# Sigmoid attention and a gated MLP on one core: 24 sums of token halves made by GpSimd instead of VectorE

## The chip, the cores and the metric

The kernel runs on one core of a Trainium2 chip. The metric is the device time of one execution in microseconds. The core's engines work through their own lists of instructions in order, and wait for each other by semaphores: TensorE (PE in the profile, with its weight loads as PEld), VectorE (DVE), ScalarE (ACT), GpSimd (POOL) and SyncE (SP), which here issues the stores.

## The reference

For 8 batches, 12 heads, 448 tokens and a head dimension of 64, attention with a sigmoid in place of the softmax is followed by a gated MLP on 3584 tokens of width 768, with a hidden width of 2048:

```
scores = q @ k.T / sqrt(64) - log(448)
x      = sigmoid(scores) @ v                # heads side by side: 3584 x 768
h      = x @ w_in                           # 3584 x 2048
g      = h * sigmoid(beta * h)
out    = g @ w_out                          # 3584 x 768, float32
```

## The kernel before

**Tiling.** Attention works on groups of 4 heads of one batch (24 groups, g = 3b to 3b+2 for batch b). Scores are made transposed (keys on partitions), ScalarE takes the sigmoid out of PSUM (L225), and the products with v give x transposed, which VectorE copies as f16 into the tile `xT` of the batch (128 x 6 x 448: six blocks of 128 features by 448 tokens, L294). Layer one then gives the hidden units on partitions in `gt`, and layer two gives token tiles of 128 rows, in pairs, which SyncE stores.

**Seven products instead of eight.** For batches 2 to 7, layer one is done by a Strassen-like scheme (Winograd's form): both operands are cut into halves, sums of halves are made first, and seven products P1 to P7 replace eight. The sums of the weights (`w_S`, `w_T`) are made once. The sums of the token halves are made for every batch by `token_sum(b, i)`, four to a batch, 24 in all: each takes two f16 blocks of 128 x 672 elements (3 features' blocks by 224 tokens) from SBUF and writes a third. With b11, b12, b21 and b22 the quarters of `xT` (features by tokens) they are, in this order or with the last two exchanged:

- sum 0: t0 = b12 - b11, read by product P5
- sum 1: t1 = b22 - t0, read by P6
- sum 2: b12 = b22 - b12, in place in `xT`, read by P7
- sum 3: t2 = b21 - t1, read by P4

t0, t1 and t2 lie in the tile `xs`, of which there is one buffer: the next batch's sum 0 waits for the last readers of this batch's. Products P1, P2 and P3 read no sum made here. Layer two uses the same scheme on pairs of token tiles; its sums of hidden halves (`hidden_sum`, tile `sum`, 128 x 1024, f16) are made by VectorE from `gt`.

**Order.** The order of all work behind a short prologue is one list of steps written out by hand. Every engine gets its instructions in the order of this list. The names of the steps that matter:

- Xb.i: `token_sum` of batch b, sum i
- Ib.d.p: product p of layer one for the d-th quarter of the hidden units (L433 by way of L166), with its eviction (L453 on ScalarE, L455 to L472 on VectorE, or sigmoids L415 on ScalarE)
- Gb.d and Bb.d.j: sigmoids on ScalarE (L415) and then the gate's product on GpSimd (L482 and L492), which writes `gt`
- Ht.i: `hidden_sum` on VectorE; Ut.p.part: half of product p of layer two for the tiles t and t+1, with its eviction
- Qg and Kb: loads of q and k of a group (two transfers) and of v of a batch (six), all issued by GpSimd (L110, L131, L138)
- Vg.j: scores of a group and their sigmoids; Ag: the product with v and its two copies into `xT`; Rg.r: transposes of q and k on VectorE; Eb: a copy of rows of v on VectorE

The stretch of the list around batch 5's first sums:

```
        V18.2 I4.3.4 B4.3.1 X5.0 A17 B4.3.0 I5.0.1 G4.3 Q21 X5.1 U14.1.0 V18.1 I5.0.2 I5.0.6 U14.1.1
        I5.0.5 V18.0 U14.2.0 H14.0 H14.1 I5.0.3 H14.2 U14.2.1 X5.2 X5.3 V18.3 U14.6.0 E6 U14.6.1
```

**PSUM.** In this part four banks are shared by all products of TensorE but the scores. `bank` takes the bank that has been free longest in the order of the list, so a product that opens a bank waits for the eviction that emptied it: I7.0.5 takes the one that U20.3.1 leaves, and U18.1.0 the one of U16.4.1.

**Helper.** `add` (L361, L362) is the VectorE operation on two inputs behind the sums of weights, of tokens and of hidden halves, and behind most evictions. In the profile all of them have the line L362, and are told apart by their tiles.

Of the kernel before, what the change touches and what calls it, by code (L numbers as in the profile page):

```python
# [13 lines left out]
def kernel(  # L14
# [10 lines left out]
    nc = tc.nc  # L25
    AF = mybir.ActivationFunctionType
    ALU = mybir.AluOpType
# [333 lines left out]
    def add(out, in0, in1, op=ALU.add):  # L361
        nc.vector.tensor_tensor(out=out, in0=in0, in1=in1, op=op)  # L362
# [36 lines left out]
    def token_sum(b: int, i: int):  # L399
        x = xTs[b]  # L400
        b11, b12 = x[:, 0:NK, 0:QH], x[:, 0:NK, QH:S]
        b21, b22 = x[:, NK:NHC, 0:QH], x[:, NK:NHC, QH:S]
        if i == 0:
            xs[b] = xsp.tile([P, 3, NK, QH], FP16, tag="xs", name="xs")
        t = xs[b]
        out, in0, in1 = (
            (t[:, 0], b12, b11),
            (t[:, 1], b22, t[:, 0]),
            (b12, b22, b12),
            (t[:, 2], b21, t[:, 1]),  # L410
        )[i]
        add(out, in0, in1, ALU.subtract)

    def sigmoid(out, in_, dc: int):
        nc.scalar.activation(  # L415
# [181 lines left out]
    def first_half(n: int):  # L597
# [13 lines left out]
        "Q": load_qk,  # L611
        "K": load_v,
        "X": token_sum,
        "G": weigh_right,
        "B": weigh_below,
# [74 lines left out]
    with tc.manual_schedule():  # L690
# [6 lines left out]
        for r, c0, c1 in early:  # L697
# [3 lines left out]
                out=staged[r],  # L701
# [113 lines left out]
```

## Time and profile before

| what | value |
|---|---|
| median of 3 runs | 372.45 us (372.42 to 374.46) |
| the profiled execution | 372.17 us, of it the span from first to last instruction 370.4 us |
| TensorE busy | 363.1 us (98%) |
| VectorE busy | 271.2 us (73%) |
| ScalarE busy | 246.9 us (67%) |
| GpSimd busy | 147.7 us (40%), 186 instructions |
| the 24 token sums on VectorE | 12.1 us, about 0.5 us each |
| the 52 hidden sums on VectorE | 37.7 us, 0.68 us each as a rule |
| the 72 gate products on GpSimd | 81.6 us, 1.14 us each |

Busy time is the union of an engine's instructions. A group's row gives its line, engine, operation and tiles (output, arrow, inputs), shapes, count, then busy time and mean duration in nanoseconds, and the idle time just before its instructions with what ended it. A row of the timeline gives start and duration in microseconds from the start of the span, and then the same names; instructions of one kind that follow each other are merged, with their count. What an engine waited for stands in brackets.

### The profile page before, as it was taken

What the parts mean: (1) busy time and instruction counts of PE and PEld (TensorE: products, weight loads), DVE (VectorE), ACT (ScalarE), POOL (GpSimd) and SP (SyncE); (2) the same over time, 40 slices, a digit from 0 to 9 for tenths busy, and PEclk for the clock granted to TensorE, in tenths of its full rate; (3) what the DMA queues carried; (4) which work ended last, traced back from release to release, by engine and by line L of the source; (5) the groups of instructions that cost most, each with busy time, mean ns of one, the idle gap of its engine ahead of it and who ended that gap; (6) DMA issues with size and microseconds to landing.
All of it is one profiled execution on the core that took longest, in us unless ns stands there. A gap on an engine that the chain in (4) does not pass through costs nothing.

```text
span 370.4 us, 9145 instructions
## 1 busy us (share of the span) xinstructions
PE 363.1 (98%) x3699; PEld 234.8 (63%) x3699; DVE 271.2 (73%) x513; ACT 246.9 (67%) x403; POOL 147.7 (40%) x186
## 2 busy tenths in 40 slices
PE   8999999999999999999999999999999999999996
PEld 2477754444465685647856678668656587669754
DVE  4356757878897697866989668768879577966774
ACT  5987985689667586666975669939776688215410
POOL 7834523151104478023750177556712136123710
PEclk9999999999999999999999999999999999999999
DMA  8999999857240943918433093328333120033004
GB/s 168 183 196 201 199 205 198 185 78 98 47 92 1 176 86 52 131 29 153 85 50 87 2 160 53 51 44 119 51 52 85 23 67 2 8 79 85 3 22 150
DMA packets 42698, 34.76 MB, mean 94 GB/s; under 512 B 21904, under 2 KB 39200, under 8 KB 42656
## 3 DMA queue, kind: packets, MB, share of 16 engines
q0 software_dynamic: 36688, 22.47, 44.3%
q1 hardware_dynamic: 5968, 11.71, 12.0%
q8 instruction: 29, 0.48, 0.5%
q14 instruction: 13, 0.11, 0.1%
HBM read 45.62 MB, written 11.01 MB: 153 GB/s over the span
## 4 chain that ended last, share of the span: by engine, by line
PE 83%; DMA 7%; POOL 4%; DVE 2%; ACT 2%; issue 1%; SPq 0%; POOLq 0%; ACTq 0%; DVEq 0%
PE m_ps L166 66%; PE sco L213 10%; PE av_ps L285 8%; DMA w_in<-in_moe_w_in_dram 3%; DMA out_dram<-osb 2%; POOL gt L492 2%; DMA raw<-in_k_dram 2%; DVE sum L362 1%; POOL w_in L148 1%; DVE osb L362 1%; ACT attnT L225 1%; POOL raw L110 1%; ACT sg L415 0%; SPq L592 0%; ACT osb L453 0%
## 5 line engine op out<-in xcount | busy, mean ns | idle before, releaser
L225 ACT ACTIVATE attnT<-sco 128x896 f16<-128x896 f32 (+1 forms) x163 | 139.3, 909 | 52.0 <-PE sco L213 51.4
L362 DVE TENSOR_TENSOR osb<-m_ps,osb 128x448 f32<-128x448 f32 (+2 forms) x187 | 110.2, 596 | 43.6 <-PE m_ps L166 36.9
L166 PEld LDWEIGHTS <-w_in 128*128 128x128 f16 (+1 forms) x960 | 80.8, 100 | 22.5 <-issue 10.9
L166 PE MATMUL m_ps<-xT,w_in 128*128 128x224 f16 (+3 forms) x768 | 90.7, 272 | 0.2 <-DMA w_in<-in_moe_w_in_dram 0.2
L492 POOL TENSOR_TENSOR gt<-osb,sg 128x448 f16<-128x448 f32 x48 | 54.0, 1142 | 64.5 <-ACT sg L415 64.4
L482 POOL TENSOR_TENSOR gt<-osb,sg 128x448 f16<-128x448 f32 x24 | 27.6, 1150 | 83.7 <-ACT sg L415 66.0
L166 PEld LDWEIGHTS <-sum 128*128 128x128 f16 (+1 forms) x496 | 40.2, 102 | 30.0 <-issue 4.6
L415 ACT ACTIVATE sg<-osb,beta_sb 128x448 f32<-128x448 f32 (+1 forms) x96 | 49.4, 575 | 13.5 <-DVE osb L362 13.5
L166 PE MATMUL m_ps<-w_out,gt 128*128 128x384 f16 (+2 forms) x348 | 52.8, 323 | 0.7 <-DVE osb L557 0.7
L166 PEld LDWEIGHTS <-gt 128*128 128x128 f16 (+1 forms) x476 | 36.9, 102 | 25.8 <-issue 8.9
L213 PE MATMUL sco<-qT,kT 32*128 32x448 f16 (+3 forms) x864 | 51.7, 339 | 0.8 <-DVE kT L199 0.6
L166 PEld LDWEIGHTS <-w_S 128*128 128x128 f16 (+1 forms) x444 | 40.8, 98 | 6.3 <-issue 4.6
L166 PE MATMUL m_ps<-w_T,sum 128*128 128x384 f16 (+1 forms) x252 | 40.3, 327 | 0.7 <-DVE sum L362 0.7
L166 PE MATMUL m_ps<-w_out,sum 128*128 128x384 f16 (+1 forms) x244 | 40.8, 327 | 0.1
L294 DVE CAST xT<-av_ps 128x448 f16<-128x448 f32 (+1 forms) x54 | 28.4, 567 | 15.8 <-PE av_ps L285 15.7
L285 PE MATMUL av_ps<-attnT,v 128*64 128x448 f16 (+3 forms) x400 | 38.2, 343 | 0.0
L314 DVE TENSOR_TENSOR gt<-m_ps,sg 128x224 f16<-128x224 f32 (+1 forms) x48 | 21.5, 465 | 16.2 <-ACT sg L311 15.3
L166 PE MATMUL m_ps<-xs,w_S 128*128 128x224 f16 (+1 forms) x294 | 32.9, 259 | 0.0
L285 PEld LDWEIGHTS <-v 128*64 128x64 f16 (+1 forms) x432 | 20.4, 108 | 17.9 <-issue 9.8
L110 POOL DMA_DIRECT2D raw<-in_q_dram x26 | 15.0, 578 | 36.4 <-DVE qT L191 20.9
L213 PEld LDWEIGHTS <-kT 32*128 32x128 f16 (+1 forms) x864 | 13.7, 96 | 24.5 <-issue 21.1
L311 ACT ACTIVATE sg<-m_ps,beta_sb 128x224 f32<-128x224 f32 (+1 forms) x48 | 23.4, 525 | 5.9 <-PE m_ps L166 2.0
(50 smaller groups left out, 297.9 us busy)
## 6 DMA issues: line engine op xcount, KB each, us to landing
out_dram<-osb SPq DMA_DIRECT2D x100, 96.0 KB, 1.9
raw<-in_k_dram POOLq DMA_DIRECT2D x23, 224.0 KB, 5.0
raw<-in_q_dram POOLq DMA_DIRECT2D x21, 224.0 KB, 3.9
v<-in_v_dram POOLq DMA_DIRECT2D x32, 144.0 KB, 6.5
w_in<-in_moe_w_in_dram POOLq DMA_DIRECT2D x8, 384.0 KB, 10.8
w_out<-in_moe_w_out_dram POOLq DMA_DIRECT2D x4, 768.0 KB, 13.1
v<-in_v_dram POOLq DMA_DIRECT2D x16, 48.0 KB, 6.0
out_dram<-osb SPq DMA_DIRECT2D x4, 192.0 KB, 1.9
```

The lines of the kernel that those rows point to most:

```text
L110: nc.gpsimd.dma_start(out=raws[g][:, r, c0:c1].rearrange("p c d -> p (c d)"), in_=(q, k)[r][b, HQ * t : HQ * (t + 1)].rearrange("h (p c) d ...
L166: nc.tensor.matmul(to[c : c + step], hidden[:, c : c + step], weights, **({} if step == P else {"tile_position": (0, c)}), **flags,)
L213: nc.tensor.matmul(sco[base : base + nk, hh, u0 : u0 + n], kT[g][lo : lo + BLK, jt * P : jt * P + nk, e], qT[g][lo : lo + BLK, c0 : c0 + n ...
L225: nc.scalar.activation(out=at[:, :, 0:n], in_=sco[:, :, 0:n], func=AF.Sigmoid, bias=NEG_LOG_S, scale=MSCALE,)
L285: nc.tensor.matmul(av[hh * D : (hh + 1) * D, 0:n], vs[b][base : base + nk, 2 * (s % NPAIR) + hh, jt], at[base : base + nk, hh, 0:n], start ...
L294: nc.vector.tensor_copy(out=xTs[b][:, s % NPAIR, c0 : c0 + n], in_=av[:, 0:n])
L311: nc.scalar.activation(out=sg[:, 0:n], in_=m1[:, 0:n], func=AF.Sigmoid, bias=0.0, scale=beta_sb[:, dc : dc + 1])
L314: nc.vector.tensor_tensor(out=gt[:, dc, off : off + n], in0=m1[:, 0:n], in1=sg[:, 0:n], op=ALU.mult)
L362: nc.vector.tensor_tensor(out=out, in0=in0, in1=in1, op=op)
L415: nc.scalar.activation(out=out, in_=in_, func=AF.Sigmoid, bias=0.0, scale=beta_sb[:, dc : dc + 1])
L482: nc.gpsimd.tensor_tensor(out=gt[:, 2 * d : 2 * d + 2, off : off + QH], in0=ob[:, 0], in1=sg, op=ALU.mult)
L492: nc.gpsimd.tensor_tensor(out=gt[:, dc, off : off + S].rearrange("p (h n) -> p h n", h=2), in0=oa[:, :, j], in1=sg, op=ALU.mult,)
```

## The change

`token_sum` no longer calls the helper on VectorE; it issues the same subtraction on GpSimd. Operands, shapes, types and the list of steps are the same. GpSimd's list thereby has 24 more entries, each at the place of its step among the gate products and the loads, and VectorE's has 24 fewer. The places where the sums wait for their inputs, and where others wait for the sums, stay, with GpSimd as the engine that waits and is waited for.

```diff
@@ -409,7 +409,7 @@
             (b12, b22, b12),
             (t[:, 2], b21, t[:, 1]),
         )[i]
-        add(out, in0, in1, ALU.subtract)
+        nc.gpsimd.tensor_tensor(out=out, in0=in0, in1=in1, op=ALU.subtract)
 
     def sigmoid(out, in_, dc: int):
         nc.scalar.activation(
```

## The prediction

> **What bounds the kernel now.** I read the page's busy times, then the groups of L362, L482 and L492, then the timelines around each of the 24 sums. The page first:
>
> ```profile
> PE 363.1 (98%) x3699; PEld 234.8 (63%) x3699; DVE 271.2 (73%) x513; ACT 246.9 (67%) x403; POOL 147.7 (40%) x186
> ...
> PE 83%; DMA 7%; POOL 4%; DVE 2%; ACT 2%; issue 1%; SPq 0%; POOLq 0%; ACTq 0%; DVEq 0%
> ```
>
> TensorE is the bound: of 370.4 us it is idle 7.3, nearly all before the first and after the last matmul; the longest hole between is 0.72 us. So relief elsewhere can win little, while any matmul that waits is lost in full, since TensorE runs its list in order. The question is whether a sum comes too late for a matmul, or delays something that does. The groups by shape give prices:
>
> ```profile
> L362 DVE TENSOR_TENSOR xs<-xT,xs 128x672 f16<-128x672 f16 x12 | 6.1, 511 | 0.2
> L362 DVE TENSOR_TENSOR xs<-xT 128x672 f16<-128x672 f16 x6 | 3.0, 501 | 0.0
> L362 DVE TENSOR_TENSOR xT<-xT 128x672 f16<-128x672 f16 x6 | 3.0, 495 | 0.0
> ...
> L492 POOL TENSOR_TENSOR gt<-osb,sg 128x448 f16<-128x448 f32 x48 | 54.0, 1142 | 64.5 <-ACT sg L415 64.4
> ```
>
> The first three are the 24 sums, 12.1 us of VectorE. The last is the only kind of two-input arithmetic that GpSimd does here. I put the steps (X5.1: batch 5's second sum) to instructions by counting what each step issues per engine; the counts fit the trace throughout.
>
> **Price of one sum on GpSimd.** The trace has none of 672 f16 elements. Products of 448 stand 1.10 us apart when back to back; by elements a sum is 1.10 x 672/448 = 1.65 us. By bytes of an input (1344 against 1792) it would be 0.83; by the mean of 1.14 us, 1.72. I take 1.65, since both are the same two-input operation over elements, and keep 0.83 and 1.72 for the range. The Trainium skill ("GPSIMD Engine Reference", Elementwise — side-by-side cycle accounting) gives about 2.6 cycles an element at 1.2 GHz: an estimate of 1.46 us, by which the sum below would be 10.8 instead of 13.4 us.
>
> **Removed.** VectorE loses 12.1 us. TensorE hardly waits for VectorE, so I cost this at a gain of 0 (at most the 0.53 and 0.72 us holes).
>
> **Moved: GpSimd's list is in order.** X now stands between G and B (gate products) and Q and K (loads). GpSimd doesn't look past a waiting head: before 211.60 it idles 20.6 us for a sigmoid while K6 stands behind, whose buffer was last read at 187.7. The worst place is batch 5, whose steps read B4.3.1 X5.0 A17 B4.3.0 I5.0.1 G4.3 Q21 X5.1 U14.1.0 V18.1 I5.0.2 I5.0.6. In the timelines of GpSimd and TensorE:
>
> ```profile
> 232.27 2.49 POOL L492 TENSOR_TENSOR gt<-osb,sg 128x448 f16<-128x448 f32 x2 [1.09 <-ACT sg L415]
> 234.73 1.13 POOL L482 TENSOR_TENSOR gt<-osb,sg 128x448 f16<-128x448 f32 x1
> 235.81 0.60 POOL L110 DMA_DIRECT2D raw<-in_q_dram  x1
> 236.40 0.54 POOL L110 DMA_DIRECT2D raw<-in_k_dram  x1
> ...
> 234.31 0.74 PE L166 MATMUL m_ps<-xs,w_S 128*128 128x224 f16 x6
> ```
>
> The first row is B4.3.1 and B4.3.0, then come G4.3 and Q21's two issues; the last is I5.0.6, which reads X5.1 (done at 233.77 on VectorE). After: B4.3.1 ends at 233.4 as now; X5.0 1.65, B4.3.0 1.10, G4.3 1.10, Q21 1.13, X5.1 1.65, so 240.0. I5.0.6 starts about 0.1 later: **5.8 us lost**. Even a free sum leaves 2.4, from the three entries ahead.
>
> **Added: GpSimd and VectorE exclude each other** when both read two SBUF operands. The rows, two on VectorE (steps H6.1, H10.0), then the GpSimd products over them:
>
> ```profile
> 142.61 1.60 DVE L362 TENSOR_TENSOR sum<-sum,gt 128x1024 f16<-128x1024 f16 x1
> ...
> 188.92 1.60 DVE L362 TENSOR_TENSOR sum<-gt 128x1024 f16<-128x1024 f16 x1
> ...
> 142.53 1.14 POOL L482 TENSOR_TENSOR gt<-osb,sg 128x448 f16<-128x448 f32 x1 [0.68 <-ACT sg L415]
> ...
> 188.84 1.14 POOL L482 TENSOR_TENSOR gt<-osb,sg 128x448 f16<-128x448 f32 x1
> ```
>
> The hidden sum (0.68 alone) ends 0.55 us after the product, both times: it waited. The other way, B4.3.0 above took 1.40 because X5.1 ran until 233.77, though B4.3.0 was next in line: a waiting VectorE goes first. Operations with one operand in PSUM (evictions) show no such stretch. So each sum on GpSimd can hold an H step for up to 1.65 us, and evictions queue behind it. Batch by batch, with 1.65:
> - Batch 2: X2.1 is ready at 103.3 behind H4.0 (until 103.85), ends 105.45; I2.0.6 wants 105.04. Then Q11 and X2.2 until 108.2; I2.0.7 wants 107.45. Together **0.8**.
> - Batch 3: X3.0 starts at 141.8, just ahead of H6.0 (141.88). H6.0 ends 144.0, G2.3 145.0, H6.1 145.55 (now 144.21). U6.6.0, at 144.27, reads H6.1: **1.35**. X3.1 is then done at 148.3, before I3.0.6 (148.8).
> - Batch 4: H10.0 ends 190.53; X4.0 follows until 192.1 and holds H10.1 until 192.65 (now 191.25). U10.6.0 (191.31) loses **1.45**, and H12.0's wait for X4.2 some **0.15** more.
> - Batch 6: X6.1 ends 277.2, just in time for I6.0.6 (277.30). X6.3 starts at 278.85, 0.1 ahead of H18.0, and holds it to 280.5; the eviction of U16.4.1 behind it ends at 281.6 (now 280.08), and U18.1.0 (280.29) needs its PSUM bank: **1.35**. This is a close race; a longer sum would lose it and cost nothing.
> - Batch 7: X7.0 can't start before G6.3 ends (317.05). H20.3, X7.1, X7.3, H22.0, X7.2 and H22.2 then alternate until 324.95; U20.3.1's eviction ends at 325.5 (now 322.94). I7.0.5 (323.04) needs that bank: **2.5**.
>
> **The sum:** 0.8 + 1.35 + 1.6 + 5.8 + 1.35 + 2.5 = 13.4 us. The profiled execution took 372.17 (span 370.4 and 1.8 around it), 0.3 below the median of the runs, which I neglect: **385.5**.
>
> **Loads moved behind sums, at nothing.** Q11 goes from 86.6 to about 105.5, lands some 4 us later, is transposed at 117.6; Q12 from 98.1 to 110.4, needed at 123.3; Q15 and K5 from 143.6 to about 152, needed at 160.0 and 191.3; Q19 by 8 us, needed at 209.2. Their cover is these margins, all over 3 us; without it a delay would pass on 1 to 1.
>
> **Rivals.**
> - **Cheap sum** (0.83 us). Batch 5: 233.4 + 3.3 + 1.7, so 4.1 lost; batches 3 and 4 0.7 each; the rest fit. 5.5 in all, so 377.7. For: f16 halves the bytes. Against: an operation over elements, and the products already write f16. Chance 0.17.
> - **The clock falls after the long wait.** At the start the nine idle matmuls come 0.43 us apart for 4 us, later ones 0.21, the page's clock column reading 1.00 throughout:
>
> ```profile
> 1.19 4.00 PE L717 MATMUL idle_ps<-gt 128*128 128x512 f16 x9 [1.19 <-DVE gt L710]
> ...
> 6.31 1.04 PE L717 MATMUL idle_ps<-gt 128*128 128x512 f16 x4
> ```
>
>  So TensorE begins at half speed. If 5.8 us without a matmul brings this back once, 4 us at half speed cost 2.0: 387.5. No hole here is over 0.72 us after that, so the trace can't say. Chance 0.32. The Trainium skill ("TensorE: Matmul & The Clock Gate", The HAM clock gate) states this rule, with an idle window of about 3.4 us; no run here shows it yet.
> - **Not slower.** GpSimd takes sums as soon as their inputs are there, ahead of waiting products: X5.0 in the hole 231.2 to 232.3, X5.1 at 233.2. It decides from the point where X5.1 is done by 234.2, a sum of 1.0 us or less; then the H steps' delays stay under their margins and VectorE's relief gains up to 1.2: 371 to 373. Against it speaks the 20.6 us idle at a waiting head. Chance 0.05.
> - **It doesn't move the work**: the sums stay on VectorE, 372.2. Chance 0.01; the call names the engine.
>
> **Numbers.** Forecast 385.5, chance 0.45. No change within 1% (3.7 us, about what a measurement of this kernel can tell) is held by the last two, so faster 0.02, same 0.04, slower 0.94. The range reaches from the cheap sum (377.5) to the clock's case with sums of 1.72 and their longer holds (389.5).
>
> **What would show it.** On GpSimd 24 subtractions of about 1.65 us; TensorE's idle time grows by the sum, with its longest hole before I5.0.6 (near 240 us, about 6 us, ended by GpSimd); hidden sums of 2 us and more under them; U6.6.0 and U10.6.0 waiting for VectorE, U18.1.0 and I7.0.5 for an eviction. Matmuls spaced twice as far behind the hole would be the clock. Sums of 1 us, or loads that TensorE's chain waits for, would make it wrong.

## The result, and the profile after

The changed kernel takes **388.47 us** (median of 4 runs, 386.32 to 388.94), the kernel before 373.12 in the same comparison: a ratio of **1.041** (95% interval 1.038 to 1.044). The forecast was 385.5 with a range of 377.5 to 389.5. The profiled execution took 386.32, the least of the four, with a span of 384.5.

The page of the changed kernel, and its table of GpSimd's groups with shapes kept apart (busy us, mean ns, idle before):

```profile
PE 365.0 (95%) x3699; PEld 235.3 (61%) x3699; DVE 274.8 (71%) x489; ACT 246.9 (64%) x403; POOL 184.8 (48%) x210
```

```profile
L412 POOL TENSOR_TENSOR xs<-xT,xs 128x672 f16<-128x672 f16 x12 | 18.5, 1541 | 9.9 <-DVE xT L294 9.5
...
L412 POOL TENSOR_TENSOR xT<-xT 128x672 f16<-128x672 f16 x6 | 10.1, 1688 | 0.0
...
L412 POOL TENSOR_TENSOR xs<-xT 128x672 f16<-128x672 f16 x6 | 9.2, 1538 | 12.5 <-DVE xT L294 12.5
```

GpSimd has 24 more instructions and 37 us more work. VectorE has 24 fewer, yet it is busy 3.6 us longer. The reason stands in its hidden sums, here of the changed kernel (before, in the same order: 18.6, 9.8 and 9.3 us):

```profile
L362 DVE TENSOR_TENSOR sum<-gt 128x1024 f16<-128x1024 f16 x26 | 23.2, 894 | 6.3 <-POOL gt L492 6.3
...
L362 DVE TENSOR_TENSOR sum<-sum,gt 128x1024 f16<-128x1024 f16 x13 | 15.0, 1152 | 0.2
...
L362 DVE TENSOR_TENSOR sum<-gt,sum 128x1024 f16<-128x1024 f16 x13 | 11.5, 886 | 0.0
```

What TensorE's matmuls waited for, by the list of waits (total us, times, longest):

```profile
PE m_ps L166 <- POOL xs L412: 5.1, 1, 5.1
...
PE m_ps L166 <- DVE sum L362: 4.1, 3, 1.7
PE m_ps L166 <- DVE osb L362: 3.6, 4, 1.6
```

Before, the first and the third of these were not there, and the second was 0.7. By this list a token sum itself comes late once, by 5.1 us; the other 7 us come by way of VectorE. To place them, the table compares the start of each step's first matmul in both profiles, and lists the steps at which the distance between the two grows:

| batch | step that starts late | growth, us | forecast, us |
|---|---|---|---|
| 2 | I2.0.6, I2.0.7, I2.0.3 | 0.19, 0.18, 1.36, of which 0.22 comes back | 0.8 |
| 3 | U6.6.0 | 1.14 | 1.35 |
| 4 | U10.6.0 | 1.14 | 1.6 |
| 5 | I5.0.6 | 5.22 | 5.8 |
| 5 | U14.1.1, I5.0.5, V18.0 | 0.50, 0.63, 0.44 | a rival, 2.0 |
| 6 | U16.6.0 | 1.41 | none |
| 6 | U18.1.0 | 0.74 | 1.35 |
| 7 | I7.0.5 | 1.77 | 2.5 |
| sum | | 14.5 | 13.4 without the rival |

The distance at the last step is 14.1 us, the span's growth as well; the missing 0.4 is mostly a first stage that in this execution ran 0.34 us earlier. I2.0.3 waits 1.19 us for an eviction of VectorE that stands behind H4.1, and H4.1 is held over two sums (X2.2 and X2.3), in the timelines of VectorE and GpSimd of the changed kernel:

```profile
106.27 3.14 DVE L362 TENSOR_TENSOR sum<-sum,gt 128x1024 f16<-128x1024 f16 x1
```

```profile
105.96 1.48 POOL L412 TENSOR_TENSOR xT<-xT 128x672 f16<-128x672 f16 x1
107.38 1.47 POOL L412 TENSOR_TENSOR xs<-xT,xs 128x672 f16<-128x672 f16 x1
```

The place of the largest loss, in the timelines of GpSimd and TensorE of the changed kernel:

```profile
235.72 1.14 POOL L492 TENSOR_TENSOR gt<-osb,sg 128x448 f16<-128x448 f32 x1 [1.08 <-ACT sg L415]
236.81 1.46 POOL L412 TENSOR_TENSOR xs<-xT 128x672 f16<-128x672 f16 x1
238.22 1.14 POOL L492 TENSOR_TENSOR gt<-osb,sg 128x448 f16<-128x448 f32 x1
239.31 1.14 POOL L482 TENSOR_TENSOR gt<-osb,sg 128x448 f16<-128x448 f32 x1
240.38 0.59 POOL L110 DMA_DIRECT2D raw<-in_q_dram  x1
240.97 0.54 POOL L110 DMA_DIRECT2D raw<-in_k_dram  x1
241.52 1.47 POOL L412 TENSOR_TENSOR xs<-xT,xs 128x672 f16<-128x672 f16 x1
```

```profile
237.24 0.75 PE L166 MATMUL m_ps<-xT,w_in 128*128 128x224 f16 x6
243.04 1.28 PE L166 MATMUL m_ps<-xs,w_S 128*128 128x224 f16 x6 [5.05 <-POOL xs L412]
244.12 1.48 PE L166 MATMUL m_ps<-w_out,gt 128*128 128x384 f16 x4
245.40 1.18 PE L166 MATMUL m_ps<-xs,w_S 128*128 128x224 f16 x6
246.51 0.58 PE L213 MATMUL sco<-qT,kT 32*128 32x448 f16 x8
247.02 0.82 PE L166 MATMUL m_ps<-w_out,gt 128*128 128x384 f16 x4
```

The list of the forecast is there entry by entry: B4.3.1, X5.0, B4.3.0, G4.3, Q21's two issues, X5.1, then I5.0.6. Behind the hole four layer-two matmuls take 1.48 us, and 0.82 three us later. The clock granted to TensorE is what differs. The windows of the same kernel (length; busy time of PE, PEld, DVE, ACT and POOL; then the granted clock as a share of full speed, and two columns on transfers) show it at 0.50:

```profile
240.00:243.00 3.00, 0.00 (x0) 0.00 (x0) 0.00 (x0) 0.00 (x0) 2.99 (x5) 0.98 0.43 59
243.00:244.00 1.00, 0.96 (x6) 0.76 (x6) 0.00 (x0) 0.00 (x0) 1.00 (x1) 0.50 1.12 195
...
246.00:247.00 1.00, 1.00 (x12) 0.38 (x10) 0.64 (x2) 0.00 (x0) 0.00 (x0) 0.85 0.03 8
247.00:248.00 1.00, 1.00 (x12) 0.73 (x9) 0.96 (x3) 0.88 (x2) 0.00 (x0) 1.00 0.00 0
```

### The profile page after: what moved, and what is told of

The parts are those of the page before. It is cut to its first block, busy times and chain, and to the rows that moved or that the text cites. A ratio compares the mean times of both kernels' runs of the same rounds, so it can differ in the third digit from the quotient of the medians.

```text
span 384.5 us, 9131 instructions
## 1 busy us (share of the span) xinstructions
PE 365.0 (95%) x3699; PEld 235.3 (61%) x3699; DVE 274.8 (71%) x489; ACT 246.9 (64%) x403; POOL 184.8 (48%) x210
## 4 chain that ended last, share of the span: by engine, by line
PE 77%; DVE 6%; POOL 5%; ACT 5%; DMA 3%; issue 3%; SPq 0%; ACTq 0%; DVEq 0%; POOLq 0%
PE m_ps L166 59%; PE sco L213 10%; PE av_ps L285 7%; DVE sum L362 4%; POOL gt L492 3%; ACT attnT L225 3%; DMA out_dram<-osb 2%; DVE osb L362 2%; ACT sg L415 1%; PE idle_ps L717 1%; DMA gt<-in_k_dram 1%; POOL xs L412 1%; POOL gt L482 1%; ACT osb L415 0%; SPq L592 0%
## 5 line engine op out<-in xcount | busy, mean ns | idle before, releaser
L166 PEld LDWEIGHTS <-w_S 128*128 128x128 f16 (+1 forms) x444 | 41.3, 100 | 15.2 <-issue 13.4
L166 PE MATMUL m_ps<-xs,w_S 128*128 128x224 f16 (+1 forms) x294 | 33.9, 264 | 6.7 <-POOL xs L412 5.1
L362 DVE TENSOR_TENSOR sum<-gt 128x1024 f16<-128x1024 f16 x26 | 23.2, 894 | 6.3 <-POOL gt L492 6.3
```

Of the source, the lines that this page charges most:

```text
L166: nc.tensor.matmul(to[c : c + step], hidden[:, c : c + step], weights, **({} if step == P else {"tile_position": (0, c)}), **flags,)
```

## The experiments

Three causes are to be told apart: the order of GpSimd's list (batch 5), the exclusion of GpSimd and VectorE (the other batches), and the clock. The common rival is that each sum on GpSimd simply costs its share, wherever it stands.

### The change again

No edit.

> The changed kernel unaltered, beside the next three on one chip. Profile and times as before: 386 to 389 us, the mean granted clock between 0.990 and 0.996, TensorE's longest hole some 5 us before the product that reads batch 5's second sum. If the spread between 386.3 and 388.9 comes from how long the clock stays at half after that hole, the time falls as the mean clock rises: 0.004 of clock is one spell of 3.1 us at half speed and 1.5 us lost, 0.010 is 7.7 us at half and 3.9 lost. Rival: the time varies by loads or otherwise, and the clock doesn't order the runs.

Measured: 387.78 us (386.99 to 389.17), before on the same chip 372.09; a ratio of 1.041 (1.035 to 1.046). The profiled execution shows the same steps late by the same amounts, I5.0.6 by 5.23, but 2.40 us of half clock behind it, at a mean clock of 0.990. The rival about the spread is right: the two executions at a clock of 0.990 took 387.0 and 387.2, those at 0.996 took 389.2 and 388.3. The clock doesn't order them, though in the first comparison the execution at 0.996 was the fastest. The spell at half clock lasts 3.41 us in the first profile and 6.83 in this one, where it begins 1.66 us before the hole's end. One other source of the spread is visible: the first stage, ahead of the steps touched here, moves by up to 2 us from one profiled execution to another. What makes up the rest of the spread stays open.

### Batch 5 back on VectorE

```diff
-        nc.gpsimd.tensor_tensor(out=out, in0=in0, in1=in1, op=ALU.subtract)
+        engine = nc.vector if b == 5 else nc.gpsimd
+        engine.tensor_tensor(out=out, in0=in0, in1=in1, op=ALU.subtract)
```

> Batch 5's four sums go back to VectorE, the other 20 stay on GpSimd. Queue theory (batch 5's second sum comes late behind B4.3.0, G4.3 and Q21, and the clock falls in the hole): 5.2 us and the clock's 1.6 to 3.9 go, 379.5 to 381.5 us, mean clock 1.000, with the losses of batches 2, 3, 4, 6 and 7 unchanged (about 7.3). Rival (each sum on GpSimd costs about the same): a sixth of the 15.4 us goes, 385.9.

Measured: 380.61 us (380.23 to 381.59), 7.2 less than the change on the same chip, and a mean clock of 1.000. Four of 24 sums carry almost half of the loss. The other batches lose what they lost: U6.6.0 1.14, U10.6.0 1.14, U16.6.0 1.41, I7.0.5 1.75.

### Batch 5 alone on GpSimd

The same edit with `b != 5`.

> Only batch 5's four sums are made by GpSimd, the other 20 by VectorE. Queue theory: the hole of 5.2 us before I5.0.6 and 1.6 to 2.4 us of half clock behind it, nothing else: 7 to 8 us over the kernel before. Rival (each sum costs about the same): a sixth of 15.5, 2.6 us over it.

Measured: 379.44 us (378.97 to 381.04), 7.2 over the kernel before (372.23). I5.0.6 starts 5.28 later and the steps behind it lose 2.2 more at half clock. The two halves add up: 8.5 and 7.2 against the change's 15.7.

### The second sum moved up in GpSimd's list

```diff
-        V18.2 I4.3.4 B4.3.1 X5.0 A17 B4.3.0 I5.0.1 G4.3 Q21 X5.1 U14.1.0 V18.1 I5.0.2 I5.0.6 U14.1.1
+        V18.2 I4.3.4 B4.3.1 X5.0 A17 X5.1 B4.3.0 I5.0.1 G4.3 Q21 U14.1.0 V18.1 I5.0.2 I5.0.6 U14.1.1
```

> All 24 sums on GpSimd; in the list of steps X5.1 is moved up from behind Q21 to behind A17, so GpSimd makes it right after X5.0, and B4.3.0, G4.3 and Q21 after it. No other engine's list changes. Queue theory: X5.1 ends 2.9 us after B4.3.1, the hole before I5.0.6 shrinks from 5.1 to about 2.0 us, too short for the clock to fall: 3.2 and 1.6 to 3.9 us go, 381.5 to 383.7 us, mean clock 1.000. Rival (the work on GpSimd, not its order, costs the time): 388. Second rival (the clock falls in a hole of 2 us too): 385, clock 0.99.

Measured: 384.90 us (384.48 to 386.12), 2.9 less than the change. The hole shrinks as the queue theory says, from 5.05 to 1.86 us, with no work taken from GpSimd. But I expected the clock to hold through it, and it didn't in three of four executions (0.996, the fourth 1.000). TensorE's timeline of this kernel:

```profile
239.34 0.75 PE L166 MATMUL m_ps<-xT,w_in 128*128 128x224 f16 x6
241.94 0.91 PE L166 MATMUL m_ps<-xs,w_S 128*128 128x224 f16 x6 [1.86 <-POOL xs L412]
242.65 1.49 PE L166 MATMUL m_ps<-w_out,gt 128*128 128x384 f16 x4
243.93 1.33 PE L166 MATMUL m_ps<-xs,w_S 128*128 128x224 f16 x6
```

The four layer-two matmuls take 1.49 us again: the second rival was right. Besides, H14.0 now falls upon X5.2 and X5.3, and U14.6.0 loses 0.93.

### The hole filled with matmuls

```diff
             m2s[key] = bank("m1_ps", S, key)
+            if (b, d, p) == (5, 0, "P6"):
+                for _ in range(22):
+                    nc.tensor.matmul(
+                        m2s[key], S1[:, 0, 0:P], w_in16[:, 0, 0:S], start=True, stop=True
+                    )
```

> As the change, with 22 more matmuls of 448 columns whose results are overwritten, put on TensorE ahead of I5.0.6: they fill about 4.1 of the 5.1 us for which it waits for X5.1. The wait itself stays. Clock theory: mean clock 1.000, and the matmuls behind the hole run at full speed: the change's time less 1.6 to 3.9 us, 384.5 to 385.0. Rival (the slow matmuls behind the hole come from something else than TensorE's idleness): as the change, 386.3 to 388.9, or a little longer for the added matmuls.

Measured: 385.95 us (385.49 to 386.32), 1.8 less than the change on the same chip, mean clock 0.999 to 1.000. TensorE's timeline of this kernel:

```profile
238.33 4.32 PE L436 MATMUL m_ps<-w_in,w_S 128*128 128x448 f16 x22
243.57 0.73 PE L166 MATMUL m_ps<-xs,w_S 128*128 128x224 f16 x6 [0.92 <-POOL xs L412]
244.15 0.81 PE L166 MATMUL m_ps<-w_out,gt 128*128 128x384 f16 x4
```

I5.0.6 is as late as ever (5.24 more), but behind it everything runs at full speed: 0.73 and 0.81 us where the change has 1.28 and 1.48. So the slow stretch comes from TensorE's idleness. The time is 1 us over what I expected: in the profiled execution 0.88 us is lost anew at I5.2.2. That product waits 0.71 us for a copy on ScalarE, and the copy waited 1.36 us for a store to land; why the store was late is open. The 1.8 us are thus what is left of the clock's 1.57 to 2.40 after such losses.

### Two entries of GpSimd's list moved

X3.0 to behind G2.3, Q19 to ahead of X4.0 (the other steps are as they were):

```diff
-        U6.1.0 H6.2 B2.3.0 X3.0 U6.1.1 V11.2 U6.7.0 U6.2.0 H6.0 H6.1 G2.3 U6.2.1 A11 X3.1 V12.0
+        U6.1.0 H6.2 B2.3.0 U6.1.1 V11.2 U6.7.0 U6.2.0 H6.0 H6.1 G2.3 X3.0 U6.2.1 A11 X3.1 V12.0
...
-        H10.1 G3.3 V15.0 E5 I4.0.1 U10.2.0 U10.7.0 U10.2.1 V15.1 U10.6.0 U10.6.1 U10.5.0 H10.3 X4.0
+        H10.1 G3.3 V15.0 E5 I4.0.1 U10.2.0 U10.7.0 U10.2.1 V15.1 U10.6.0 U10.6.1 U10.5.0 H10.3 Q19 X4.0
```

> All 24 sums on GpSimd. In the list of steps X3.0 goes from ahead of G2.3 to behind it, and Q19 goes from behind X4.2 to ahead of X4.0, so that GpSimd starts X3.0 after H6.1's wait for G2.3 and X4.0 after H10.1 has begun (about 0.5 us later). Lock theory: U6.6.0 and U10.6.0 lose no more (1.14 us each): 2.3 us under the change; if X4.3 and X4.2, now 1.1 us later, hold H12.0 and the eviction behind it, about 1.1 of that come back before I4.0.5. Rival (the two losses come from GpSimd's load, wherever the sums stand): the change's time.

Measured: 388.26 us (386.8 to 391.23), no gain. One half held: U6.6.0 starts no later than before. The other went the wrong way: U10.6.0 loses 1.84 instead of 1.14. VectorE's and GpSimd's timelines of this kernel:

```profile
190.63 1.60 DVE L362 TENSOR_TENSOR sum<-gt 128x1024 f16<-128x1024 f16 x1
192.27 2.53 DVE L362 TENSOR_TENSOR sum<-sum,gt 128x1024 f16<-128x1024 f16 x1
```

```profile
192.21 0.55 POOL L110 DMA_DIRECT2D raw<-in_k_dram  x1
192.76 1.49 POOL L412 TENSOR_TENSOR xs<-xT 128x672 f16<-128x672 f16 x1
```

By the steps the two moves are worth 0.4 us together, less than the runs of one kernel differ by. H10.1 begins 0.49 us before X4.0 by the records, and still waits until X4.0 is over, ending 0.55 us behind it. By the records, then, "begun first" is not what decides here: when the hidden sum begins, GpSimd is at a load's issue with the sum next in its list. The unforecast loss of batch 6 in the changed kernel looks the same: H16.1 begins while GpSimd issues a load, 0.31 us before X6.0, and takes 2.34 us.

```profile
278.79 2.34 DVE L362 TENSOR_TENSOR sum<-sum,gt 128x1024 f16<-128x1024 f16 x1
```

```profile
279.10 1.48 POOL L412 TENSOR_TENSOR xs<-xT 128x672 f16<-128x672 f16 x1
```

### Fills in place of the sums

```diff
-        nc.gpsimd.tensor_tensor(out=out, in0=in0, in1=in1, op=ALU.subtract)
+        for _ in range(2):
+            nc.gpsimd.memset(out, 0.0)
```

> As the change, but each of the 24 sums is replaced by two fills of its output with zeros on GpSimd, at the same place of the list: the sums are left out, GpSimd stays busy there (how long a fill of 672 takes no run shows yet; with 0.7 us each the load is the change's) and reads nothing. The fills wait for no copy of x. Lock theory (VectorE and GpSimd exclude each other only where both read from SBUF): no hidden sum over 1.65 us other than behind gate products, and the losses of batches 2, 3, 4, 6 and 7 (7.3 us) go; batch 5 keeps its hole, 3.9 to 5.2 us by the fills' length, and the half clock: 6 to 8 us over the kernel before. Rival (it is GpSimd's being busy, or its list, not its reads): losses of batches 3, 4, 6 and 7 stay, 13 to 16 us over it.

Measured: 378.66 us (378.49 to 379.54), 6.25 over the kernel before (372.41). The sums are left out and zeros written instead. A fill takes 0.66 us, two of them 1.32, nearly a sum's length. Batch 5 keeps its hole (I5.0.6 5.03 later, then 1.5 of half clock), and the losses of batches 2, 3, 4, 6 and 7 are gone; at I2.2.2 a new 0.64 appears, behind a copy on ScalarE that waits for a store, and 0.59 of it has come back by U6.6.0. VectorE's hidden sums in this kernel:

```profile
L362 DVE TENSOR_TENSOR sum<-gt 128x1024 f16<-128x1024 f16 x26 | 18.6, 717 | 6.3 <-POOL gt L493 6.3
L362 DVE TENSOR_TENSOR sum<-gt,sum 128x1024 f16<-128x1024 f16 x13 | 9.2, 704 | 0.0
L362 DVE TENSOR_TENSOR sum<-sum,gt 128x1024 f16<-128x1024 f16 x13 | 8.9, 687 | 0.2
```

They are back to 36.7 us, from 49.7 in the changed kernel; the only ones over 0.70 us are two that stand behind gate products, as before the change. GpSimd is busy at the same places of its list, and its reads are gone (with them its waits for the copies of x). Ten hidden sums run while a fill does; nine of them take 0.65 to 0.69 us, the tenth is one of the two behind gate products. So the reads hold VectorE up. The Trainium skill ("SBUF — State Buffer", Who interferes with whom) says this: VectorE with two inputs from SBUF contends with a GpSimd instruction that reads SBUF, not with one that only writes. This run agrees: 0.69 us at most beside fills alone, against up to 3.14 beside sums in the changed kernel. The page adds that whichever starts first gets the shared ports; by recorded starts H10.1 and H16.1 above don't follow that.

### Batches 2 and 3 on GpSimd, with two entries moved

Batches 4 to 7 on VectorE; X3.0 behind G2.3 as above, and Q11 behind X2.2:

```diff
-        A8 V9.2 H4.0 U2.3.1 U2.4.0 I2.0.1 X2.1 U2.4.1 Q11 I2.0.6 X2.2 H4.1 I2.0.5 V9.0 U4.1.0 X2.3
+        A8 V9.2 H4.0 U2.3.1 U2.4.0 I2.0.1 X2.1 U2.4.1 I2.0.6 X2.2 Q11 H4.1 I2.0.5 V9.0 U4.1.0 X2.3
```

> Batches 2 and 3 on GpSimd with two entries of its list moved (Q11 from ahead of X2.2 to behind it, so that X2.2 and X2.3 no longer stand back to back before H4.1; X3.0 behind G2.3), batches 4 to 7 on VectorE. Theory: the time hangs on where the sums stand, not on how many there are: 0 to 0.4 us over the kernel before. Rival (each sum on GpSimd costs 0.64 us): 5.1 us over it.

Measured: 372.14 us (10 runs) against 372.23: a ratio of 1.0005 (0.9985 to 1.0026). Eight sums on GpSimd cost nothing where they stand well, and gain nothing either, though VectorE has eight sums of 0.5 us less to make (its busy time is 269.7 us, before 271.2).

### All 24 sums on GpSimd, with batches 2, 3 and 5 moved

As above for batches 2 and 3, and in batch 5 X5.0 ahead of B4.3.1 and X5.1 right behind A17.

> All 24 sums on GpSimd, with the two moves for batches 2 and 3, and in batch 5 X5.0 ahead of B4.3.1 and X5.1 right behind A17, so that GpSimd does X5.0 while B4.3.1's sigmoid is not ready. Theory: batch 2 loses 0.2 us, 3 nothing, 4 1.1, 5 about 0.95 (and 0 to 1.5 of half clock), 6 2.15, 7 1.75: 6 to 8 us over the kernel before, 8 to 9 under the change. Rival (load, not place): the change's time.

Measured: 381.32 us (380.43 to 383.44), 9.1 over the kernel before and 6 to 7 under the change: more than expected. Batches 2 and 3 lose nothing beyond 0.2, I5.0.6 only 0.78. But a new wait has come, in the timelines of VectorE, GpSimd and TensorE of this kernel:

```profile
238.76 4.12 DVE L362 TENSOR_TENSOR sum<-gt 128x1024 f16<-128x1024 f16 x1
```

```profile
238.87 0.55 POOL L110 DMA_DIRECT2D raw<-in_k_dram  x1
239.41 1.49 POOL L412 TENSOR_TENSOR xT<-xT 128x672 f16<-128x672 f16 x1
240.83 1.48 POOL L412 TENSOR_TENSOR xs<-xT,xs 128x672 f16<-128x672 f16 x1
```

```profile
243.65 1.91 PE L166 MATMUL m_ps<-w_T,sum 128*64 128x384 f16 x16 [2.45 <-DVE sum L362]
```

H14.0 begins during Q21's issue and is held over both X5.2 and X5.3; U14.6.0 loses 2.5 us and the clock falls again (the steps behind it lose 1.7). Moving the sums forward in GpSimd's list put X5.2 and X5.3 in VectorE's way.

## Why the prediction was right

The direction and the place hold, by the mechanisms that were forecast. The size holds in part by luck. At the measured 1.46 us a sum, the prediction itself gives 10.8 us. In the table, the rows it priced too high came out 2.6 us smaller together (batches 3, 4, 5, U18.1.0 and 7), and losses that it had too small or not at all came out 2.1 larger (batch 2 and U16.6.0), so that the steps add up to 12.9 without the clock against 13.4. The clock's 1.57 us, a rival in the forecast, come on top.

- **The price of a sum.** Forecast 1.65 us, scaled by elements from the products; measured 1.46 where nothing holds it. The Trainium skill's estimate of 1.46 ("GPSIMD Engine Reference", Elementwise — side-by-side cycle accounting) is what the trace shows. By element a sum costs less than a product does (1.46 us for 672 against 1.10 for 448). Whether the products have a fixed part that scaling by elements took along, or their f32 inputs cost more, no run here tells. The price of a sum is the term that was mis-sized: it is most of the reason why batch 5 loses 5.22 instead of 5.8, and it makes batches 3, 4 and 7 smaller too.
- **The order of GpSimd's list.** Right entry by entry, and shown by the second sum moved up (5.05 to 1.86 us) and by batch 5 alone (7.2 us).
- **The clock after the wait.** Forecast as a rival with a chance of 0.32 and 2.0 us. It happens: 1.57 and 2.40 us in two profiled executions, and filling the hole takes 1.8 us off the median. With it the forecast's own rows would have given 387.5, nearer to the 388.47 measured. I had set the point where it begins too high: I thought of a hole of 5 us, and one of 1.86 did it.
- **The exclusion.** That it would cost TensorE by way of the hidden sums and of evictions was right, as the fills show. The rule that I used for who goes first was wrong. I took from one row that a waiting VectorE goes ahead of GpSimd's next instruction, and that the one that begins first keeps the ports. In batch 2, H4.1 was held over X2.2 and X2.3 (3.14 us), so most of the loss lies at I2.0.3 (1.36), behind the eviction that waited for it, and little at I2.0.6 and I2.0.7 (0.19 and 0.18), where the forecast had all of it; batch 6's H16.1 was held by an X6.0 that began later (1.41, not forecast).
- **No gain from VectorE's relief.** Right: eight sums moved without loss change the time by a ratio of 1.0005.
- **Loads at nothing.** Right: behind the first token sum no product of TensorE waits for a load in the changed kernel's timeline.

The rivals that fell: the cheap sum (0.83 us), and that GpSimd takes a sum ahead of a waiting product.

## What to carry to other kernels

Work moved to an idle engine is priced by its place in that engine's list, not by its length: add up what stands between the moment its inputs are there and its turn, and compare with the reader's start in the old trace. Then look for what the moved work shares with the engine that was relieved; here both read SBUF through something they can't use together, and the relieved engine got slower. Where the bound engine is TensorE and it waits for some 2 us or more, allow for a spell at half clock behind the hole.

## What the runs showed of the hardware that was not expected

- A hole of 1.86 us on TensorE was enough for half clock in three of four executions, and the spell then lasted 3.41 us by the granted clock, as long as the one at the hole of 5.05 us in the changed kernel's first profile. The Trainium skill ("TensorE: Matmul & The Clock Gate", The HAM clock gate) gives an idle window of about 3.4 us ahead of it; these runs show it after a shorter hole.
- The records of the granted clock show a pattern. In the seven profiled executions whose clock falls behind batch 5's hole, it falls 67 to 70 times 3.41 us after its first rise, and stays at half for 3.41 us (four times) or 6.83 (three times). If each of the eleven profiles is cut into stretches of 3.41 us from that rise on, every stretch at full clock with 1.86 us or more without matmuls is followed by a fall, and no stretch with up to 1.71 us is. The hole of 1.86 us lay whole within one stretch in the profile; that in the fourth execution it lay across two is a guess, as it has no trace. A spell costs about half of the part of it that lies behind the hole (3.26 us, and 1.57 lost, in the changed kernel's first profile).
- A hidden sum on VectorE that began while GpSimd issued a load waited, at three places (H16.1, H10.1 and H14.0 above), for the arithmetic behind that load, begun 0.31 to 0.65 us later. Where GpSimd stood idle, beginning first was enough: in the changed kernel H4.0, begun 0.23 us before X2.1, took its 0.68 us, and X2.1 took 1.77. Sum 2 followed by sum 3 (X2.2 and X2.3, X5.2 and X5.3) held it for both: 3.14 and 4.12 us instead of 0.68. In the other order (X3.3 and X3.2, for one) VectorE came in between, and X3.2 took 1.91 us; so it did where a sum needed the one before it and stood 0.08 us behind. What grants the ports can't be told from recorded starts and stays open.
- Fills on GpSimd, which read nothing, don't hold VectorE's hidden sums (0.69 us at most beside fills alone).
